# Batch 1's keys pooled by GpSimd, a new order of all steps, and no dummy matmuls, in a pooled attention and FFN kernel on one Trainium2 core

## The chip, the core and the metric

The kernel runs on one core of a Trainium2 chip. The time is the device time of one execution in microseconds (us). The engines have their own queues and run each its instructions in the order of the program: TensorE (PE, with its weight loads PEld), VectorE (DVE), ScalarE (ACT), GpSimd (POOL) and SyncE (SP, which issues the DMAs). They wait for one another by semaphores.

## The reference

Eight batches of 576 tokens with 8 heads of 64. Keys and values are pooled by means of 8, which leaves 72 of each. Softmax attention gives x; then x is normalized and goes through two matrix products with a ReLU between, and x is added.

```python
k_p = k.reshape(B, H, Sp, pool, D).mean(axis=3)
v_p = v.reshape(B, H, Sp, pool, D).mean(axis=3)
scores = scale * np.matmul(q, k_p.transpose(0, 1, 3, 2))
scores = scores - np.max(scores, axis=-1, keepdims=True)
attn = np.exp(scores)
attn = attn / (np.sum(attn, axis=-1, keepdims=True) + 1e-09)
attn_out = np.matmul(attn, v_p)
x = attn_out.transpose(0, 2, 1, 3).reshape(B, S, H * D)
mu = np.mean(x, axis=-1, keepdims=True)
var = np.mean((x - mu) ** 2, axis=-1, keepdims=True)
xn = (x - mu) / np.sqrt(var + 1e-06) * g_ln
ch = np.maximum(xn @ w_ch1, 0.0) @ w_ch2        # 512 -> 2048 -> 512
return x + ch
```

## The kernel before

The 4608 tokens are 36 tiles of 128, and 9 chunks of four tiles. For each tile, step A loads q, multiplies it with the pooled keys of the tile's batch (or of its two batches: tile 4 holds the end of batch 0 and the start of batch 1) and takes the row maxima (matmuls L788 into `ps_a`, DVE L798). For tiles 0 to 3 the steps E compute the same scores turned, half a tile at a time (PE L847 and L854, ACT exponentials L859 and L860), and POOL takes the low part of the probabilities (L862); for later tiles DVE subtracts the maxima (L803), ACT takes the exponentials, and POOL makes the low part (L824, L827). Step B multiplies the probabilities with the pooled values (matmuls L923 to L925, for later tiles L927 and L928), and DVE makes x and its mean and variance of it (L935, L943, L945, L955, L956). Then x is turned by matmuls (`parts_turned`, L876 and L884 into `ps_m`), ACT scales the result into a high part (L894) and a full copy `z` (L897), and POOL subtracts the two for the low part (L899).

Numbers that need more precision than f16 are kept as a high and a low f16 part, and a product is then three matmuls. The weights w1 and w2 are converted so in eight blocks each: C converts (ACT L532, L536, DVE L540), M1 and M2 find the scales, and S splits a block (ACT L480 the high part, DVE L487 the low one; for the first four blocks of w2 ACT L482 and POOL L484).

F is a sixteenth of a chunk's first product (`ffn_in`, L1111) with ACT and DVE making its ReLU's two parts (L1120, L1122); G is one tile of the second product (`ffn_out`, L1314, with DVE L1325 adding it to x). From chunk 2 on the first product, and from chunk 3 on the second, is done by a scheme with seven products of quarters in place of eight (`product` L1155, `out_seven` L1272); T, U, TW, WH, KW, EL, ER, ES, EP and LW make and load the sums and the parts which that scheme needs.

HK and HV load half a batch's keys and values and pool them, a pair of heads or a head at a time. `pool_k` has two branches. Keys of a batch in `K_GPSIMD` come from DRAM with the pooled index outermost, and POOL adds 4 to 4, 2 to 2 and 1 to 1 (L648, L649, two L656 straight into `kblk`); other keys are reduced by DVE (L652) and copied into `kblk` by DVE (two L658). The host lays out `kT` by the same table (L1437). Values are added by POOL (L672 to L674).

Nothing is scheduled by a planner: two strings of tokens, START and STEADY, say in which order the steps go. Each step is a generator; `run()` advances a token's generator by one stage whenever the token comes up, so the order of tokens is the order of instructions on every engine at once, and of the DMAs. START ends in chunk 1's second product; with it the first PSUM pools are closed (`ps_s` 1 buffer for scores, `ps_x` 1 for values, `ps_f` 3, `ps_m` 1).

`KEEP_BUSY` = {2: 12}: ahead of the third call of `parts_turned` (tile 2's x) 12 matmuls of the identity with itself go into the same PSUM tile (L872), which the real matmuls then overwrite.

Of the kernel before, what the change touches and what calls it, by code (L numbers as in the profile page):

```python
# [67 lines left out]
E.2.1 B.0 B.1 S.1.0 S.1.0 S.1.1 C.2.0 HK.1.0 HK.1.0 R.2.2 R.2.2 C.1.3 C.1.3 E.2.1 E.2.1 E.2.0 E.2.0 HV.1.0 HV.1.0 A.3
HK.1.1 HV.1.1 A.3 A.3 A.3 S.1.1 S.1.1 C.1.2 C.1.2 B.0 B.0 E.3.0 E.3.1 B.0 E.3.0 S.1.2 E.3.1 A.4 B.1 B.1 B.1 B.2 B.0 B.0
B.1 HK.1.0 HK.1.0 S.1.2 S.1.2 S.1.3 C.2.1 C.2.2 B.2 B.2 B.2 E.3.0 E.3.0 E.3.1 E.3.1 B.3 B.1 B.1 B.2 S.1.3 S.1.3 F.0.0.0  # L70
F.0.1.0 F.0.2.0 F.0.0.0 F.0.1.0 HK.1.1 HK.1.1 R.2.3 R.2.3 C.2.1 C.2.0 C.2.0 C.2.0 C.2.1 C.2.1 F.0.2.0 C.2.3 HK.1.1
HK.1.1 A.4 F.0.0.0 F.0.0.0 F.0.3.0 F.0.1.0 F.0.1.0 F.0.4.0 A.4 A.4 F.0.4.0 F.0.2.0 F.0.2.0 C.2.2 C.2.3 B.3 B.3 HV.1.1
HV.1.0 HV.1.0 HV.1.1 HK.2.0 A.5 D.0 D.0 A.5 F.0.5.0 B.3 F.0.5.0 F.0.3.0 C.2.2 C.2.2 C.2.3 C.2.3 B.2 B.2 B.3 HV.1.1
HV.1.1 R.1.4 R.1.4 A.4 F.0.4.0 F.0.4.0 F.0.3.0 F.0.3.0 F.0.6.0 F.0.7.0 F.0.6.0 HV.1.1 HV.1.1 A.4 A.4 R.1.5 R.1.5 R.1.6
R.1.6 R.1.7 R.1.7 A.5 A.5 F.0.7.0 F.0.5.0 F.0.5.0 B.3 B.3 M2.0 M2.0 F.0.0.1 M2.0 M2.0 S.2.0 F.0.0.1 F.0.6.0 F.0.6.0
F.0.1.1 F.0.1.1 HV.1.1 F.0.7.0 F.0.7.0 HV.1.1 HV.1.1 F.0.2.1 HV.1.1 HV.1.1 F.0.2.1 F.0.0.1 F.0.0.1 F.0.1.1 F.0.1.1
HV.1.1 HV.1.1 HV.1.1 D.1 D.1 HV.2.0 A.5 S.2.0 S.2.0 F.0.2.1 F.0.2.1 HK.2.0 HK.2.0 A.6 A.6 F.0.3.1 F.0.4.1 A.6 C.1.5
C.1.5 S.2.1 F.0.3.1 F.0.4.1 A.6 C.1.6 S.2.1 S.2.1 S.2.2 F.0.3.1 F.0.3.1 C.1.4 F.0.4.1 F.0.4.1 C.1.7 A.6 M1.1 S.2.2
S.2.2 HV.2.0 HV.2.0 A.5 A.5 HK.2.1 A.7 A.7 F.0.5.1 F.0.6.1 B.4 F.0.7.1 M1.1 F.0.5.1 C.1.4 S.2.3 F.0.6.1 F.0.7.1 C.1.6
C.1.7 A.7 A.7 C.1.5 C.1.5 F.0.5.1 F.0.5.1 C.1.4 C.1.4 R.2.4 R.2.4 A.6 A.6 R.2.5 R.2.5 S.2.3 S.2.3 B.4 F.0.6.1 F.0.6.1  # L80
HK.2.0 HK.2.0 B.4 A.7 HK.2.1 HK.2.1 HV.2.0 HV.2.0 A.8 A.8 G.0.0.0 B.5 G.0.1.0 G.0.0.0 G.0.0.0 M1.1 M1.1 S.1.4 C.2.4 B.5
B.6 F.0.7.1 F.0.7.1 G.0.2.0 G.0.3.0 C.1.7 C.1.7 S.1.4 S.1.4 S.1.5 C.2.5 C.1.6 C.1.6 R.2.6 R.2.6 C.2.4 S.1.5 S.1.5 S.1.6
C.2.4 C.2.4 G.0.1.0 G.0.1.0 A.8 A.8 HK.2.1 HK.2.1 S.1.6 S.1.6 S.1.7 C.2.6 B.4 HV.2.0 HV.2.0 R.2.7 R.2.7 HV.2.1 A.7 A.7
C.2.7 B.6 G.0.2.0 G.0.2.0 A.8 S.1.7 S.1.7 HV.2.0 HV.2.0 B.4 HV.2.1 HV.2.1 B.4 B.4 B.5 HV.2.1 HV.2.1 A.8 A.8 HV.2.1
HV.2.1 A.9 A.9 F.0.8 F.0.8 A.10 HV.3.0 A.9 A.10 F.0.9 B.7 A.11 C.2.6 C.2.6 C.2.6 C.2.5 C.2.5 C.2.5 C.2.7 C.2.7 C.2.7
F.0.9 B.5 A.9 G.0.3.0 G.0.3.0 F.0.10 F.0.10 F.0.8 F.0.8 M2.1 M2.1 F.0.11 F.0.11 B.7 B.8 F.0.9 F.0.9 F.0.12 F.0.10
F.0.10 A.9 A.9 A.9 M2.1 M2.1 S.2.4 F.0.12 HV.2.1 A.10 A.11 B.5 HV.2.1 HV.2.1 F.0.13 S.2.4 S.2.4 S.2.5 F.0.13 F.0.12
F.0.12 F.0.11 F.0.11 F.0.14 F.0.15 S.2.5 S.2.5 HV.2.1 HV.2.1 S.2.6 F.0.14 F.0.13 F.0.13 T.1.0 HV.2.1 HV.2.1 HV.2.1
HV.2.1 B.6 B.6 T.1.0 S.2.6 S.2.6 S.2.7 F.0.15 A.10 HV.3.0 HV.3.0 B.5 B.5 B.6 F.0.14 F.0.14 S.2.7 S.2.7 B.7 B.7 F.0.15
F.0.15 G.0.0.1 G.0.1.1 G.0.2.1 HV.3.0 HV.3.0 HK.3.0 B.6 B.6 G.0.0.1 T.1.0 B.7 HV.3.0 HV.3.0 G.0.0.1 G.0.0.1 B.7 B.7  # L90
HV.3.1 A.10 A.10 A.10 HK.3.0 T.1.0 A.11 A.11 HV.3.0 HV.3.0 G.0.1.1 G.0.1.1 G.0.1.1 T.1.0 T.1.0 T.1.0 B.8 B.9 G.0.3.1
HV.3.1 HV.3.1 G.0.2.1 G.0.2.1 G.0.2.1 A.11 HV.3.1 HV.3.1 A.11 A.11 B.9 V.10 F.1.0 HV.3.1 HV.3.1 HK.3.0 HK.3.1 V.10 B.11
F.1.1 F.1.1 F.1.0 T.1.0 G.0.3.1 G.0.3.1 G.0.3.1 B.8 HV.3.1 HV.3.1 HV.3.1 F.1.2 F.1.2 F.1.1 F.1.1 F.1.0 F.1.0 F.1.3
F.1.4 T.1.0 T.1.0 F.1.3 HV.3.1 F.1.2 F.1.2 F.1.5 F.1.5 F.1.4 T.1.0 T.1.0 HK.3.0 HK.3.0 T.1.1 T.1.1 F.1.3 F.1.3 F.1.6
F.1.5 F.1.5 F.1.4 F.1.4 F.1.7 T.1.1 T.1.1 T.1.1 T.1.1 F.1.6 F.1.7 B.8 T.1.1 T.1.1 F.1.7 F.1.7 F.1.6 F.1.6 G.1.0.0
G.1.1.0 G.1.2.0 T.1.1 T.1.1 T.1.1 T.1.1 G.1.0.0 G.1.0.0 G.1.3.0 T.0.0 T.0.0 T.0.0 T.0.0 T.0.0 T.0.0 HV.3.1 T.0.0 T.0.0
T.0.0 T.0.0 T.0.0 T.0.0 T.0.1 T.0.1 G.1.2.0 G.1.2.0 G.1.1.0 G.1.1.0 F.1.8 F.1.9 F.1.8 T.0.1 T.0.1 B.8 G.1.3.0 G.1.3.0
# [1363 lines left out]
```

## Time and profile before

| | us |
|---|---|
| median of three runs | 813.9 |
| the three runs | 811.84, 813.9, 815.95 |
| the profiled execution | 814.76 |
| its span on the core | 813.0 |
| granted TensorE clock, mean over the span | 0.998 |
| ACT busy | 470.7 (58%) |
| POOL busy | 487.6 (60%) |

A busy time is the sum over an engine's instructions, on the profiled execution. The profile's other views are cut by time: a table of stretches gives each engine's busy time in a stretch with the mean granted clock; the waits group an engine's idle time by what ended it; a group of instructions has the form "line engine operation out<-in count | busy us, mean ns | idle us before them"; a time line has "start, duration, engine, line, ..., [idle before <- what ended it]". Buffers are named without their numbers.

### The profile page before, as it was taken

Reading aid. Unit: us, or ns where it says so; the run is one execution under the profiler, and the core shown is the slowest. Engines: PE = TensorE matmul, PEld = TensorE weight load, DVE = VectorE, ACT = ScalarE, POOL = GpSimd, SP = SyncE. Lnnn points to the kernel's source line nnn. Section 1 sums busy time; section 2 is a strip of 40 time slices with the busy share of each in tenths; the row PEclk is TensorE's granted clock in tenths of the full one; section 3 lists DMA queues with packets and bytes.
Section 4 is the critical chain, followed back from the end, with each engine's and each line's share of the span. In section 5 each row is a group of like instructions: output and inputs, shape, how many; then the busy total and the mean of one; then the engine's idle time right before and its main releaser. Section 6 shows DMA issues by size and latency. Waiting matters only on the chain.

```text
span 813.0 us, 17388 instructions
## 1 busy us (share of the span) xinstructions
PE 782.8 (96%) x6618; PEld 609.5 (75%) x6618; DVE 664.0 (82%) x1352; ACT 470.7 (58%) x880; POOL 487.6 (60%) x601
## 2 busy tenths in 40 slices
...
GB/s 352 277 151 306 205 188 150 215 8 1 44 120 126 165 217 132 192 188 242 190 174 183 211 192 243 134 250 164 243 85 206 166 134 168 174 152 161 76 120 130
DMA packets 181507, 138.91 MB, mean 171 GB/s; under 512 B 143792, under 2 KB 151600, under 8 KB 179248
## 3 DMA queue, kind: packets, MB, share of 16 engines
...
q8 instruction: 52, 0.85, 0.4%
...
## 4 chain that ended last, share of the span: by engine, by line
PE 54%; DVE 6%; ACT 1%; DMA 1%; issue 1%; DVEq 0%; ACTq 0%
PE ps_f L1155 25%; PE ps_f L1272 25%; PE ps_a L788 2%; PE ps_f L1314 1%; DVE w L1193 1%; DMA ring<-w2s 1%; PE ps_a L927 1%; PE ps_a L928 1%; DVE ring L1185 1%; DVE x L1289 0%; DVE raw L1172 0%; DVE phl L1169 0%; DVE mx L798 0%; DVE raw L1013 0%; DVE raw L1169 0%
## 5 line engine op out<-in xcount | busy, mean ns | idle before, releaser
L1272 PE MATMUL ps_f<-ring,w 128*128 128x256 f16 x2016 | 231.5, 273 | 2.4 <-DVE w L1193 1.0
L1272 PEld LDWEIGHTS <-w 128*128 128x128 f16 x2016 | 196.4, 98 | 26.6 <-DVE w L1193 1.6
L1155 PE MATMUL ps_f<-zts,w 128*128 128x256 f16 x1680 | 206.7, 273 | 2.9 <-DVE raw L1169 1.4
L1155 PEld LDWEIGHTS <-w 128*128 128x128 f16 x1680 | 163.5, 98 | 23.7 <-issue 4.2
L1314 PE MATMUL ps_f<-w,ring 128*128 128x512 f16 x576 | 126.6, 379 | 2.6 <-DVE x L1325 2.2
L1174 ACT COPY raw<-ps_f 128x256 f32<-128x256 f32 x160 | 56.4, 373 | 91.4 <-PE ps_f L1155 80.8
L1314 PEld LDWEIGHTS <-ring 128*128 128x128 f16 x576 | 56.1, 98 | 68.9 <-issue 3.4
L1155 PE MATMUL ps_f<-zts,tsp 128*128 128x256 f16 x672 | 91.0, 273 | 1.7 <-ACT raw L1174 1.7
L1111 PE MATMUL ps_f<-zts,w 128*128 128x512 f16 (+1 forms) x480 | 86.9, 338 | 1.5 <-DVE w L487 1.4
L1191 ACT CAST w<-w 128x512 f16<-128x512 f32 x96 | 58.9, 618 | 44.6 <-POOL w L1211 24.5
L1193 POOL TENSOR_TENSOR w<-w 128x512 f16<-128x512 f32 x48 | 58.3, 1214 | 32.2 <-ACT w L1191 24.4
L1111 PEld LDWEIGHTS <-w 128*128 128x128 f16 x480 | 46.3, 98 | 37.8 <-DVE w L487 1.9
L1155 PEld LDWEIGHTS <-tsp 128*128 128x128 f16 x672 | 65.0, 98 | 10.1 <-issue 2.2
L1210 POOL TENSOR_TENSOR w<-raw 128x256 f32<-128x256 f32 x32 | 25.0, 780 | 65.5 <-ACT raw L1202 37.9
L1289 DVE SCALAR_TENSOR_TENSOR x<-ps_f,y,x 128x256 f32<-128x256 f32 (+1 forms) x84 | 42.0, 517 | 24.2 <-PE ps_f L1272 23.1
L824 POOL TENSOR_TENSOR phl<-e,phl 128x512 f16<-128x512 f32 x32 | 39.0, 1220 | 37.5 <-ACT phl L814 37.5
L1080 POOL TENSOR_TENSOR hl<-raw,hl 128x640 f16<-128x640 f32 x28 | 40.9, 1463 | 25.9 <-ACT hl L1078 25.8
L1289 DVE SCALAR_TENSOR_TENSOR x<-ps_f,cy,x 128x256 f32<-128x256 f32 (+1 forms) x84 | 42.2, 516 | 14.1 <-PE ps_f L1272 13.6
L1193 DVE TENSOR_TENSOR w<-raw,w 128x512 f16<-128x512 f32 (+1 forms) x64 | 45.0, 709 | 3.9 <-ACT w L1191 3.9
L788 PE MATMUL ps_a<-kblk,q 128*128 128x144 f32 (+1 forms) x320 | 43.3, 294 | 3.7 <-issue 2.5
L1169 DVE TENSOR_TENSOR raw<-ps_f,raw 128x256 f32<-128x256 f32 x80 | 32.2, 415 | 15.9 <-ACT raw L1174 9.4
L1120 ACT ACTIVATE ring<-ps_f 128x512 f16<-128x512 f32 (+1 forms) x40 | 19.4, 506 | 43.9 <-PE ps_f L1111 29.6
(182 smaller groups left out, 1480.3 us busy)
## 6 DMA issues: line engine op xcount, KB each, us to landing
...
```

The source lines that it names most:

```text
L788: nc.tensor.matmul(ps[r, p // 2, p % 2 * 2 * KV : (p % 2 + 1) * 2 * KV], lhsT=q[:, p, r], rhs=kblk[b % NKB][:, p, :], start=True, stop=True,)
L824: nc.gpsimd.tensor_tensor(out=ph[:, 0, :, KA:P], in0=e[:, :, 0:KA], in1=ph[:, 0, :, 0:KA], op=ALU.subtract)
L1080: nc.gpsimd.tensor_tensor(out=zhl[:, 1, :], in0=src, in1=zhl[:, 0, :], op=ALU.subtract)
L1111: nc.tensor.matmul(ps, lhsT=w[:, part, fs], rhs=zT[:, kz, cols], start=(n == 0), stop=(n == 3 * NKT - 1),)
L1155: nc.tensor.matmul(ps, lhsT=w[:, part, f * P : (f + 1) * P], rhs=z, start=m in (1, 2, 4, 5) and n == 0, stop=m in (2, 3, 4, 7) and n == 3 ...
L1169: nc.vector.tensor_tensor(out=o, in0=ps, in1=o, op=ALU.add)
L1174: nc.scalar.copy(out=o, in_=ps)
L1191: nc.scalar.copy(out=hi, in_=src)
L1193: engine.tensor_tensor(out=lo, in0=src, in1=hi, op=ALU.subtract)
L1272: nc.tensor.matmul(ps, lhsT=wt[2][:, left, part, f * HC + u * P : f * HC + (u + 1) * P], rhs=b[:, f // FPB, wp, f % FPB], start=n < 4 and ...
L1289: nc.vector.scalar_tensor_tensor(out=x, in0=ps, scalar=scale, in1=x, op0=ALU.mult, op1=ALU.add)
L1314: nc.tensor.matmul(ps, lhsT=h[:, part, i, cols], rhs=w[:, wp, j], start=(n == 0), stop=(n == 3 * NFT // 2 - 1),)
```

## The change

Three edits. The table `K_GPSIMD` gets batch 1 beside batch 2, in the kernel and so in the host's layout of `kT`. `KEEP_BUSY` goes, with its loop and its counter. And both strings of tokens are replaced by others that hold the same tokens, each as often as before (761 in START, 3398 in STEADY), in another order; lines below the strings move up by 4, below `parts_turned` by 11.

```diff
-KEEP_BUSY = {2: 12}
...
-K_GPSIMD, V_GPSIMD = (2,), (1, 2)
+K_GPSIMD, V_GPSIMD = (1, 2), (1, 2)
...
 START = """
-LN.2 LN.2 LK.0 LK.0 LK.1 LK.1 Q.0 Q.0 R.1.0 R.1.0 R.1.1 R.1.1 Q.1 Q.1 R.1.2 R.1.2 R.1.3 R.1.3 A.0 HV.1.0 LG LG R.2.0
...
+LN.2 LN.2 LK.0 LK.0 LK.1 LK.1 Q.0 Q.0 R.1.0 R.1.0 R.1.1 R.1.1 Q.1 Q.1 R.1.2 R.1.2 HV.1.0 HK.1.0 A.0 R.1.3 R.1.3 LG LG
...
-    n_turned = [0]
-
     def parts_turned(x, ln, cv, dst):
         ps = psum["ps_m"].tile([P, CH], F32, name="ps_m").rearrange("p (k c) -> p k c", k=NKT)
-        n_turned[0] += 1
-        for _ in range(KEEP_BUSY.get(n_turned[0] - 1, 0)):
-            nc.tensor.matmul(
-                ps, lhsT=ident, rhs=ident.unsqueeze(1).broadcast_to([P, NKT, P]), start=True, stop=True
-            )
         for k in range(NKT):
```

On PE, before, between the values matmuls of tile 2 and those of tile 3, with the twelve dummy pairs (L872) of which the last is shown, and the turned part of tile 2 (L876, L884):

```order
L872 LDWEIGHTS ident
L872 MATMUL ps_m<-ident 128x512
L876 MATMUL ps_m<-zts,x 128x128 x4
L884 MATMUL ps_m<-zts,ln 128x512
L923 LDWEIGHTS pt
L923 MATMUL ps_a<-vh,pt 128x65
```

The same place in the changed kernel, whose `kblk_113` and `kblk_114` are the pooled keys of batches 0 and 1:

```order
L843 MATMUL ps_f<-q,kblk_113 72x128
L850 MATMUL ps_f<-zts,mx 72x128
L784 MATMUL ps_a<-kblk_113,q 64x144
L784 MATMUL ps_a<-kblk_114,q 64x144
L784 MATMUL ps_a<-kblk_113,q 64x144
L784 MATMUL ps_a<-kblk_114,q 64x144
L784 MATMUL ps_a<-kblk_113,q 64x144
L784 MATMUL ps_a<-kblk_114,q 64x144
L784 MATMUL ps_a<-kblk_113,q 64x144
L784 MATMUL ps_a<-kblk_114,q 64x144
L865 MATMUL ps_m<-zts,x 128x128 x4
L873 MATMUL ps_m<-zts,ln 128x512
```

The dummies are gone; four pairs of tile 3's turned scores (the last of them shown) and all scores of tile 4 now stand ahead of tile 2's turned part, and behind it comes the first of F (L1100, before L1111).

On POOL, before, from the first low parts of the probabilities on (`phl_115` for tiles 0 and 2, `phl_116` for tiles 1 and 3):

```order
L862 TENSOR_TENSOR pt<-phl_115,pt 72x512
L862 TENSOR_TENSOR pt<-phl_116,pt 72x512 x2
L672 TENSOR_TENSOR vr<-vr 72x256
L673 TENSOR_TENSOR vr<-vr 72x128
L674 TENSOR_TENSOR vp<-vr 72x64
L672 TENSOR_TENSOR vr<-vr 72x256
L673 TENSOR_TENSOR vr<-vr 72x128
L674 TENSOR_TENSOR vp<-vr 72x64
L862 TENSOR_TENSOR pt<-phl_115,pt 72x512 x2
```

And in the changed kernel, where L858 is the old L862, L668 to L670 are the old L672 to L674, and L644, L645 and L652 are the additions of the keys:

```order
L858 TENSOR_TENSOR pt<-phl_115,pt 72x512
L668 TENSOR_TENSOR vr<-vr 72x256
L669 TENSOR_TENSOR vr<-vr 72x128
L670 TENSOR_TENSOR vp<-vr 72x64
L644 TENSOR_TENSOR kr<-kr 128x288
L645 TENSOR_TENSOR kr<-kr 128x144
L652 TENSOR_TENSOR kblk_114<-kr 64x72 x2
L858 TENSOR_TENSOR pt<-phl_116,pt 72x512
L644 TENSOR_TENSOR kr<-kr 128x288
L645 TENSOR_TENSOR kr<-kr 128x144
L652 TENSOR_TENSOR kblk_114<-kr 64x72 x2
```

The first two sets of keys, of four, stand between the low parts of tiles 0 and 1, and one set of values among them.

On DVE, before, from tile 0's x (L945) on, where L487 splits a block of w1 and L540 converts one:

```order
L945 TENSOR_TENSOR x<-ps_a,rs 128x512
L955 BN_STATS st<-x 128x6
L956 BN_AGGR ln<-st 128x2
L487 SCALAR_TENSOR_TENSOR w_90<-w_90,gs 128x1024
L652 TENSOR_REDUCE kr<-kr 128x72
L658 COPY kblk_114<-kr 64x72 x2
L540 SCALAR_TENSOR_TENSOR w_90<-w_90,ring 128x1024
L798 TENSOR_REDUCE mx<-ps_a 128x8
L487 SCALAR_TENSOR_TENSOR w_90<-w_90,gs 128x1024
```

And in the changed kernel from tile 0's x on (L934 is x, L794 the maxima, L483 the split):

```order
L934 TENSOR_TENSOR x<-ps_a,rs 128x512
L944 BN_STATS st<-x 128x6
L945 BN_AGGR ln<-st 128x2
L794 TENSOR_REDUCE mx<-ps_a 128x8
L483 SCALAR_TENSOR_TENSOR w_90<-w_90,gs 128x1024
L924 TENSOR_SCALAR sm<-ps_a,cv 128x8
L932 RECIPROCAL rs<-sm 128x8
L934 TENSOR_TENSOR x<-ps_a,rs 128x512
```

The reductions and copies of batch 1's keys are gone from DVE, and one split with one row of maxima is all that stands between the x of tile 0 and that of tile 1 (the last row).

More of the change, by code (lines that the diff above doesn't have):

```diff
@@ L68 @@
[L68 to L97, printed above, removed]
@@ new lines @@
+P.2.1.0.7 P.2.1.0.7 G.2.2.0 B.14 B.14 G.2.0.0 G.2.0.0 B.14 B.14 Z.14.0 WH.2.1.0 WH.2.1.1 HV.4.1 HK.4.1 HK.4.1 KW.0.2
+KW.0.2 TW.0.3.0 TW.0.3.0 TW.0.2.1 TW.0.2.1 HV.5.0 KW.1.2 KW.1.2 KW.1.0 KW.1.0 KW.0.0 KW.0.0 TW.0.3.1 TW.0.3.1 HK.4.1
+HK.4.1 TW.1.0.0 G.2.3.0 G.2.3.0 P.2.1.2.2 P.2.1.2.5 P.2.1.2.1 P.2.1.3.1 TW.1.0.0 G.2.1.0 G.2.1.0 P.2.1.3.2 TW.1.0.0
+TW.0.3.1 Z.14.0 Z.14.0 B.15 WH.2.1.0 WH.2.1.0 P.2.1.2.1 P.2.1.2.1 TW.0.3.1 P.2.1.2.5 P.2.1.2.5 TW.1.0.0 HV.4.1
+P.2.1.2.6 G.2.2.0 G.2.2.0 P.2.1.3.5 P.2.1.2.2 P.2.1.2.2 P.2.1.2.4 A.16 TS.3 WH.2.1.1 WH.2.1.1 P.2.1.3.1 P.2.1.3.1
@@ new lines @@
+ES.4.0.2 EP.4.0.2.0 ER.4.0.3 ER.4.0.3 B.20 P.4.1.0.7 P.4.1.0.7 O.4.0.0.1 P.4.1.1.1 EL.4.1.0 P.4.1.1.5 P.4.1.1.5 B.21
+HV.6.1 HV.6.1 HK.6.0 LW.4.0.2 LW.4.0.2 A.22 A.22 O.4.0.0.0 O.4.0.0.0 O.4.0.1.0 O.4.0.1.0 O.4.0.2.0 ES.4.0.2 ES.4.0.2
+EP.4.0.2.0 EP.4.0.2.0 O.4.0.0.1 O.4.0.0.1 O.4.0.1.1 O.4.0.1.1 O.4.0.2.1 B.22 P.4.1.1.3 ER.4.1.0 EP.4.0.2.1 HV.6.1
+HV.6.1 LW.4.0.4 LW.4.0.4 LW.4.0.6 LW.4.0.6 B.20 B.20 LW.4.0.5 LW.4.0.5 HK.6.1 ES.4.0.3 EP.4.0.3.0 HK.6.0 HK.6.0
+O.4.0.2.1 O.4.0.2.1 EP.4.0.2.1 EP.4.0.2.1 O.4.0.2.0 O.4.0.2.0 EP.4.0.3.0 EP.4.0.3.0 O.4.0.3.1 P.4.1.1.2 P.4.1.1.1
@@ new lines @@
+P.4.1.1.1 A.23 P.4.1.1.6 O.4.0.4.0 P.4.1.1.6 P.4.1.1.6 B.21 P.4.1.1.7 O.4.0.4.1 HV.6.1 ES.4.0.3 ES.4.0.3 EP.4.0.3.1
+A.23 A.23 A.23 A.24 B.22 EL.4.1.0 EL.4.1.0 P.4.1.1.2 P.4.1.1.2 P.4.1.1.4 P.4.1.1.4 P.4.1.1.4 P.4.1.1.3 P.4.1.1.3
+O.4.0.3.0 ES.4.1.0 EP.4.1.0.0 EL.4.1.1 B.21 B.21 B.21 LW.4.1.0 LW.4.1.0 LW.4.1.1 LW.4.1.1 HV.7.0 HV.6.1 O.4.0.4.1
+O.4.0.4.1 B.22 B.22 ER.4.1.0 ER.4.1.0 EP.4.0.3.1 EP.4.0.3.1 O.4.0.6.1 O.4.0.4.0 O.4.0.4.0 O.4.0.3.1 O.4.0.3.1 O.4.0.5.1
+O.4.0.6.0 B.23 P.4.1.1.7 P.4.1.1.7 ER.4.1.1 ES.4.1.0 ES.4.1.0 EL.4.1.1 EL.4.1.1 O.4.0.6.1 O.4.0.6.1 EP.4.1.0.0
```

564 lines of the change are left out of this document (288 added, 276 removed).

## The prediction

> **What bounds the kernel now.** I read the page first: its head, the busy times, then the table of stretches, the waits, and last the time lines at the waits found.
>
> ```profile
> span 813.0 us, 17388 instructions
> PE 782.8 (96%) x6618; PEld 609.5 (75%) x6618; DVE 664.0 (82%) x1352; ACT 470.7 (58%) x880; POOL 487.6 (60%) x601
> ```
>
> TensorE (PE) is busy for 782.8 of 813.0 us, so all that an unchanged amount of PE work can give back is 30.2 us. The table of stretches says where that lies (columns: stretch, then busy time and count on each engine, granted clock, DMA share, GB/s).
>
> ```profile
> core 0: us, PE busy (x) PEld busy (x) DVE busy (x) ACT busy (x) POOL busy (x), PEclk, DMA share, GB/s
> 20.00:60.00 40.00, 35.91 (x355) 30.10 (x353) 38.93 (x62) 34.35 (x50) 29.65 (x37) 1.00 0.64 214
> 60.00:100.00 40.00, 37.52 (x296) 25.15 (x296) 36.80 (x85) 35.38 (x50) 34.27 (x43) 1.00 0.82 257
> 100.00:120.00 20.00, 17.38 (x93) 9.27 (x92) 19.38 (x30) 16.96 (x25) 17.23 (x22) 0.91 0.79 195
> 111.00:114.50 3.50, 2.97 (x11) 2.36 (x12) 3.50 (x4) 3.06 (x5) 3.42 (x3) 0.51 0.49 117
> 120.00:230.00 110.00, 109.85 (x569) 51.50 (x568) 88.90 (x155) 36.22 (x60) 54.65 (x58) 1.00 0.36 85
> 230.00:330.00 100.00, 93.47 (x703) 63.28 (x701) 86.23 (x182) 45.14 (x91) 59.76 (x86) 1.00 0.69 156
> 330.00:813.00 483.00, 476.25 (x4558) 423.39 (x4556) 383.42 (x818) 295.57 (x602) 290.67 (x351) 1.00 0.64 174
> ```
>
> From 120 to 230 PE has 0.15 us of idle time: that stretch gives nothing. PE idles 4.09 us in 20 to 60, 2.48 in 60 to 100, 2.62 in 100 to 120, 6.53 in 230 to 330 and 6.75 in the last 483. From 20 to 60 VectorE (DVE) is busy 38.93 of 40 us: there it sets the pace. And for 3.5 us after 111 PE ran at a granted clock of 0.51: work done there at half speed would have taken half as long, so some 1.7 us more are lost in it.
>
> ```profile
> PE ps_a L788 <- issue: 2.5, 2, 1.3
> PE ps_m L876 <- DVE x L945: 1.7, 2, 1.2
> ```
>
> These are the two longest of PE's waits from 20 to 125 (total, times, longest). The time line has them, and one more, at two places that the change touches, the third turned part and the eighth block of w1 (the bracket gives the idle time ahead of a row and what ended it):
>
> ```profile
> 42.84 2.75 PE L872 MATMUL ps_m<-ident 128*128 128x512 bf16 x12 [0.63 <-ACT z L897]
> 46.82 1.16 PE L876 MATMUL ps_m<-zts,x 128*128 128x128 f32 x8 [1.23 <-DVE x L945]
> 109.96 0.39 PE L1111 MATMUL ps_f<-zts,w 128*128 128x512 f16 x1 [1.44 <-DVE w L487]
> 111.53 2.26 PE L788 MATMUL ps_a<-kblk,q 128*128 128x144 f32 x8 [1.18 <-issue]
> ```
>
> **The change, first 60 us.** DVE loses the four reductions and the eight copies of batch 1's keys.
>
> ```profile
> L658 DVE COPY kblk<-kr 64x72 f32<-64x72 f32 x8 | 3.3, 412 | 0.2
> L652 DVE TENSOR_REDUCE kr<-kr 128x72 f32<-128x576 f32 x4 | 2.9, 736 | 0.0
> ```
>
> That is 3.3 + 2.9 = 6.2 us off the engine that sets the pace. The x for which the third turned part waits ended just before 46.82; with some 5 us less ahead of it (what the new order puts in front of it takes back about one), it ends near 41.8.
>
> The dummies by themselves cost nothing: they filled 2.75 us of a pause that ran to 46.82 for that x. Where they go and DVE is 5 us earlier, the pause is gone as well, if PE has other work. The new order gives it: ahead of the third turned part stand half a tile of turned scores and the scores of tile 4.
>
> ```profile
> 34.77 0.38 PE L847 MATMUL ps_f<-q,kblk 128*72 128x128 f32 x2
> 36.30 0.38 PE L854 MATMUL ps_f<-zts,mx 128*72 128x128 f32 x2
> 53.48 1.38 PE L788 MATMUL ps_a<-kblk,q 128*64 128x144 f32 x16
> ```
>
> From 34.77 to 36.30 are seven steps, so a step takes 0.22 us and the eight of a half tile 1.75; the scores take 1.38. That is 3.13 us of work moved forward. If nothing holds PE, it goes through the third turned part 3.13 us after its last values matmul instead of 4.6 us after (from 42.84 - 0.63 = 42.2, the end of the values matmuls ahead of it, to 46.82), with 3.13 us of later work done.
>
> What can hold it is GpSimd (POOL). The scores of tile 4 need all of batch 1's pooled keys, and these now come from POOL, behind six subtractions L862, three sets of V additions and one L899. A key set is priced where POOL does it already, for batch 2:
>
> ```profile
> 92.83 0.80 POOL L648 TENSOR_TENSOR kr<-kr 128x288 f32<-128x288 f32 x1
> 93.70 0.48 POOL L649 TENSOR_TENSOR kr<-kr 128x144 f32<-128x144 f32 x1
> 94.27 0.72 POOL L656 TENSOR_TENSOR kblk<-kr 64x72 f32<-64x72 f32 x2
> 95.07 1.62 POOL L672 TENSOR_TENSOR vr<-vr 72x256 f32<-72x256 f32 x1
> 20.86 1.15 POOL L862 TENSOR_TENSOR pt<-phl,pt 72x512 f16<-72x512 f32 x1 [18.76 <-ACT pt L860]
> 53.55 0.73 POOL L672 TENSOR_TENSOR vr<-vr 72x256 f32<-72x256 f32 x1
> 55.15 0.36 POOL L823 MEMSET phl<- 128x320 f16 x1
> ```
>
> A set runs from 92.83 to 95.07, 2.24 us; a V set from 53.55 to 55.15, 1.6. Quiet, the queue up to the last key set is 6 x 1.15 + 3 x 1.6 + 4 x 2.24 + 1.2 = 21.9 us from 20.86, so 42.8: before PE gets there (42.2 + 1.75 = 43.95). But POOL is slower when other engines are dense:
>
> ```profile
> L862 POOL TENSOR_TENSOR pt<-phl,pt 72x512 f16<-72x512 f32 x8 | 11.0, 1392 | 21.3 <-ACT pt L860 21.3
> L672 POOL TENSOR_TENSOR vr<-vr 72x256 f32<-72x256 f32 x8 | 6.8, 848 | 0.5 <-DMA vr<-in_v_dram 0.5
> L899 POOL TENSOR_TENSOR zts<-z,zts 128x512 f16<-128x512 f32 x4 | 4.8, 1199 | 3.9 <-ACT z L897 3.9
> L673 POOL TENSOR_TENSOR vr<-vr 72x128 f32<-72x128 f32 x8 | 4.5, 566 | 0.6
> L674 POOL TENSOR_TENSOR vp<-vr 72x64 f32<-72x64 f32 x8 | 4.3, 533 | 0.6
> L648 POOL TENSOR_TENSOR kr<-kr 128x288 f32<-128x288 f32 x1 | 1.2, 1246 | 0.0
> ```
>
> These are the groups of POOL from 20 to 72. By their means an L862 takes 1.39, a V set 0.85 + 0.57 + 0.53 = 1.95, and the one L648 among them 1.246 where the quiet one took 0.80, so a key set about 3.5. The queue is then 8.4 + 5.9 + 14.0 + 1.2 = 29.5 us and ends at 50.4. The old POOL also waited 21.3 - 18.76 = 2.5 us for ScalarE in there; if that stays, it ends at 52.9.
>
> The break-even: the third turned part may start at 46.82 + 3.13 = 49.95 without loss, so the scores 1.38 earlier, at 48.6. Quiet gives 42.8, loaded 50.4. I take the middle, 46.6, since DVE, the dense neighbour, is lighter by a sixth: a gain of 2.0. Set against that is a clock halved once more as at 111, 1.7 us at one chance in three, so 0.6: about **-1.5 us**. Bounds: all idle time and the dummies' gone, -(4.09 + 2.75) = -6.8; loaded, with the wait and the half clock, 52.9 - 48.6 + 1.7 = +6.0.
>
> **60 to 120 us.** At 109.96 PE waited 1.44 us for the low part of w1's eighth block, and at 111.53 another 1.18 us for the buffer of the scores, which DVE empties; after these two the clock was 0.51. The profile names nothing for the second ("issue"), but the scores have one buffer, and it is DVE that empties it. So I put all three down to DVE being late:
>
> ```profile
> 42.45 3.22 DVE L487 SCALAR_TENSOR_TENSOR w<-w,gs 128x1024 f16<-128x1024 f32 x1
> 41.20 2.27 POOL L862 TENSOR_TENSOR pt<-phl,pt 72x512 f16<-72x512 f32 x2
> 43.43 1.15 POOL L899 TENSOR_TENSOR zts<-z,zts 128x512 f16<-128x512 f32 x1
> 108.62 1.28 DVE L487 SCALAR_TENSOR_TENSOR w<-w,gs 128x1024 f16<-128x1024 f32 x1
> ```
>
> In the new order DVE has nearly the whole 6.2 us less ahead of that split, four times the wait. At most 1.44 + 1.18 + 1.7 = 4.3 us come back. But ScalarE (35.38 of 40 us from 60 to 100) and POOL (34.27) are nearly as dense as DVE (36.80), and POOL gets the four key sets, 9 to 14 us, in return; a second product that waits for POOL's or ScalarE's parts of w2 would eat the lead. **-2.5 us**, bounds -4.3 and 0.
>
> The same lines show a price that the change raises. The split at 42.45 took 3.22 us while POOL worked through L862 and L899, the one at 108.62 took 1.28. Each addition that goes to POOL can hold up a DVE operation so; that is in the loaded end of the first term. The Trainium skill, "SBUF — State Buffer", section "Who interferes with whom", says that a DVE operation with two inputs in SBUF and a GpSimd operation that reads SBUF exclude each other for a whole instruction, while a reduction on trn2 never contends. The trace agrees in the 3.22 against 1.28. It speaks against the move: a reduction that disturbs nobody goes, and additions that block come. By it the first term would be 50.4 - 48.6 = +1.8 in place of -1.5; this is the slower rival below.
>
> **230 us to the end.** The second order table is new throughout; PE's idle time here is 6.53 + 6.75 us. The largest single wait:
>
> ```profile
> 326.95 5.34 PE L1314 MATMUL ps_f<-w,ring 128*128 128x512 f16 x24 [2.23 <-DVE x L1325]
> ```
>
> DVE is busy 86.23 of 100 us there; in the new order a little less of its work stands ahead of the densest place, 250 to 300. I take **-1 us**; bounds: most of the 6.53 gone, -5, and two more waits like this one, +4.5.
>
> **The sum.** -1.5 - 2.5 - 1 = -5.0 on the profiled execution's 814.76 us: 809.8. The median of the three times, 813.9, lies 0.86 lower, so 808.9, given as **809.0**. About 0.5% (4.1 us) is what a measurement of this kernel can tell from no change: faster means under 809.8, slower over 818.0.
>
> **The rivals.** *No change*: DVE's lead is eaten. For it: from 60 to 100 ScalarE and POOL are as dense as DVE, so that a lead of DVE is worth only what its two partners allow; against: the two longest waits name DVE. Then the first term stays and half of the second, the third is nought: 813.9 - 1.5 = about 812.5; with any half clock 814. It includes that removing the dummies does nothing, since they filled a wait. *Slower*: POOL becomes what PE waits for at tile 4's scores. For it: loaded sets end at 50.4, past the break-even of 48.6; against: POOL had idle time and DVE, which slows it, is lighter. Price: 1.8 to 4.3 us of waiting and 1.7 of half clock, and since everything behind is later too, DVE's lead at w1's eighth block is lost: 813.9 + 3.5 to 6.0, about 819. It decides from the point where key sets take over 3.0 us each with the rest as loaded (48.6 - 20.86 - 15.5 = 12.2, over four).
>
> The half clock is a part of that. PE ran at 0.51 from 111 to 114.5 after pauses of 1.44 and 1.18 us with 0.39 us of work between. The Trainium skill, "TensorE: Matmul & The Clock Gate", section "Part 1: The HAM clock gate (the "warmup" mystery)", puts the drop after an idle window of about 3.4 us; here less than that was enough. By the rule a pause of 4.6 us without dummies halves the clock for one window, and a filled one does not.
>
> **How the numbers follow.** Forecast 0.5; no change 0.33; slower 0.17. The range 803.0 to 817.5: below, the first two terms at two thirds of their bounds and the third at its middle (-4.5 - 3.5 - 3 = -11); above, the slower rival short of its middle, where a tenth is left out. The same cases give faster 0.5, same 0.33, slower 0.17.
>
> **What would show it.** Right: PE idles under 2 us from 40 to 50, its scores of tile 4 start by 46.6, L1111 does not wait for the eighth L487, and the clock stays at 1.00 to 120. Wrong: PE waits at tile 4's scores for POOL's last key addition; the clock drops near 45; L1314's first product waits for POOL's or ScalarE's part of w2; or new waits after 230 where there were none.

## The result, and the profile after

The changed kernel took 824.61 us (median of 4, 822.92 to 827.10) against 814.11 for the kernel before: a ratio of 1.0131, 95% interval 1.0101 to 1.0161. It is 10.5 us slower. The forecast was 809.0 with a range up to 817.5, so the result lies outside it, and on the other side of the kernel before. The profiled execution took 825.07 us with a span of 823.4.

The table of stretches of the changed kernel (columns as in the prediction's), with two stretches of half clock added behind:

```profile
core 0: us, PE busy (x) PEld busy (x) DVE busy (x) ACT busy (x) POOL busy (x), PEclk, DMA share, GB/s
20.00:60.00 40.00, 31.10 (x300) 26.08 (x299) 32.68 (x51) 29.76 (x41) 38.04 (x51) 0.91 0.62 215
60.00:100.00 40.00, 34.37 (x281) 25.81 (x279) 35.05 (x68) 35.23 (x52) 31.71 (x40) 0.96 0.91 252
100.00:120.00 20.00, 17.78 (x99) 8.60 (x98) 19.32 (x29) 15.42 (x19) 16.92 (x19) 1.00 0.56 169
120.00:230.00 110.00, 106.84 (x569) 50.52 (x568) 91.79 (x161) 38.70 (x66) 57.76 (x62) 1.00 0.37 86
230.00:330.00 100.00, 96.71 (x710) 63.81 (x709) 82.35 (x180) 45.09 (x90) 56.67 (x78) 1.00 0.62 149
330.00:824.00 494.00, 484.39 (x4599) 427.31 (x4596) 396.09 (x832) 296.79 (x607) 300.56 (x361) 1.00 0.62 173
48.70:55.60 6.90, 6.45 (x23) 4.23 (x24) 4.80 (x4) 4.72 (x8) 6.68 (x8) 0.51 0.36 140
82.90:86.30 3.40, 3.40 (x19) 2.42 (x17) 3.33 (x4) 3.39 (x5) 2.72 (x4) 0.50 1.13 210
```

From 20 to 60 us DVE went from 38.93 busy to 32.68, as the edit says, and POOL from 29.65 to 38.04 of 40. The engine that set the pace was relieved and another took its place; PE's busy time fell by 4.8 us. Where the 10.4 us of span went, as PE's idle time and half of the time at half clock, in each stretch:

| stretch | before | after | difference | forecast |
|---|---|---|---|---|
| 20 to 60 | 4.09 idle + 2.75 dummies | 8.90 idle + 3.4 clock | +5.5 | -1.5 |
| 60 to 120 | 5.10 idle + 1.7 clock | 7.85 idle + 1.7 clock | +2.8 | -2.5 |
| 120 to 230 | 0.15 | 3.16 | +3.0 | 0 |
| 230 to the end | 13.28 | 12.3 | -1.0 | -1 |

That is +10.3. The stretches are cut by time and not by work, so that one or two us stand in the wrong row: counted at points where both kernels have done the same matmuls (shown under "The second loss"), PE is 3.6 us late by the fourth turned part, at 60 us, and 8.2 us late 20 us further on.

PE's longest waits from 20 to 125, in the changed kernel:

```profile
PE ps_a L784 <- POOL kblk L652: 5.1, 1, 5.1
PE ps_f L1100 <- DVE ring L1111: 3.0, 2, 2.1
PE ps_a L913 <- POOL pt L858: 1.6, 1, 1.6
```

The two waits of before at this place (for x and for w1's split) are gone. Ahead of them all now stands one on POOL's last addition of batch 1's keys. Here it is on PE's time line, with the half clock behind it:

```profile
42.82 1.19 PE L784 MATMUL ps_a<-kblk,q 128*64 128x144 f32 x14
49.15 0.74 PE L784 MATMUL ps_a<-kblk,q 128*64 128x144 f32 x2 [5.14 <-POOL kblk L652]
49.82 2.08 PE L865 MATMUL ps_m<-zts,x 128*128 128x128 f32 x8
...
53.40 1.91 PE L1100 MATMUL ps_f<-zts,w 128*128 128x256 f16 x8
```

and on POOL's, from its last work ahead of that set:

```profile
42.22 0.72 POOL L668 TENSOR_TENSOR vr<-vr 72x256 f32<-72x256 f32 x1
43.02 0.45 POOL L669 TENSOR_TENSOR vr<-vr 72x128 f32<-72x128 f32 x1
43.55 1.34 POOL L670 TENSOR_TENSOR vp<-vr 72x64 f32<-72x64 f32 x1
44.84 0.18 POOL L952 COPY ln<-cv 128x2 f32<-128x2 f32 x1
44.98 1.15 POOL L888 TENSOR_TENSOR zts<-z,zts 128x512 f16<-128x512 f32 x1
46.09 0.78 POOL L644 TENSOR_TENSOR kr<-kr 128x288 f32<-128x288 f32 x1
46.95 1.35 POOL L645 TENSOR_TENSOR kr<-kr 128x144 f32<-128x144 f32 x1
48.37 0.72 POOL L652 TENSOR_TENSOR kblk<-kr 64x72 f32<-64x72 f32 x2
```

POOL has no pause in there. The set ends at 49.1: 6.3 us after the quiet sum of the prediction (42.8) and 1.3 before the loaded one (50.4). The L645 that took 1.35 stood beside a DVE split of 3.32 us; another, at 27.44 beside a reduction on DVE, took 0.49.

The second place is the time line at 82.53, in front of the other half clock: PE's product waits 2.09 us for DVE's ReLU parts.

```profile
82.53 4.45 PE L1100 MATMUL ps_f<-zts,w 128*128 128x256 f16 x24 [2.09 <-DVE ring L1111]
```

```profile
78.39 1.22 DVE L536 SCALAR_TENSOR_TENSOR w<-w,raw 128x1024 int32<-128x1024 int32 x1
79.52 2.62 DVE L483 SCALAR_TENSOR_TENSOR vb<-vp,sv,vh 72x512 f16<-72x512 f32 x1
82.06 0.74 DVE L1111 SCALAR_TENSOR_TENSOR ring<-ps_f,ring 128x256 f16<-128x256 f32 x2
```

In the second fence (DVE's time line) those parts stand behind a conversion and the split of batch 1's V.

### The profile page after: what moved, and what is told of

Its sections match the earlier page's. It is cut to its first block, busy times and chain, and to the rows that moved or that the text cites. A ratio compares the mean times of both kernels' runs of the same rounds, so it can differ in the third digit from the quotient of the medians.

```text
span 823.4 us, 17338 instructions
## 1 busy us (share of the span) xinstructions
PE 784.1 (95%) x6606; PEld 609.7 (74%) x6606; DVE 667.6 (81%) x1340; ACT 468.7 (57%) x880; POOL 503.0 (61%) x617
## 4 chain that ended last, share of the span: by engine, by line
PE 66%; DVE 24%; POOL 3%; ACT 3%; issue 2%; DMA 1%; DVEq 0%; POOLq 0%
PE ps_f L1144 25%; PE ps_f L1261 23%; PE ps_f L1303 6%; PE ps_f L1100 5%; DVE w L536 2%; PE ps_a L784 2%; DVE w L1182 2%; DVE raw L611 2%; DVE ring L1174 1%; DVE w L483 1%; DVE mx L794 1%; DVE ring L1111 1%; DVE x L1278 1%; DVE x L1314 1%; PE ps_a L916 1%
## 5 line engine op out<-in xcount | busy, mean ns | idle before, releaser
L1100 PE MATMUL ps_f<-zts,w 128*128 128x512 f16 (+1 forms) x480 | 88.9, 344 | 6.8 <-DVE ring L1111 4.7
L1182 POOL TENSOR_TENSOR w<-w 128x512 f16<-128x512 f32 x48 | 59.4, 1238 | 48.2 <-ACT w L1180 30.3
L1100 PEld LDWEIGHTS <-w 128*128 128x128 f16 x480 | 48.0, 101 | 45.1 <-issue 8.4
L784 PEld LDWEIGHTS ps_a<-kblk,q 128*128 128x128 f32 (+1 forms) x320 | 37.4, 180 | 11.4 <-POOL kblk L652 5.4
L1182 DVE TENSOR_TENSOR w<-raw,w 128x512 f16<-128x512 f32 (+1 forms) x64 | 42.1, 660 | 3.0 <-ACT w L1180 3.0
```

What stands on the lines that cost most here:

```text
L784: nc.tensor.matmul(ps[r, p // 2, p % 2 * 2 * KV : (p % 2 + 1) * 2 * KV], lhsT=q[:, p, r], rhs=kblk[b % NKB][:, p, :], start=True, stop=True,)
L1100: nc.tensor.matmul(ps, lhsT=w[:, part, fs], rhs=zT[:, kz, cols], start=(n == 0), stop=(n == 3 * NKT - 1),)
L1182: engine.tensor_tensor(out=lo, in0=src, in1=hi, op=ALU.subtract)
```

## The experiments

The first theory of the loss was that the four key sets overfill POOL's queue, so that all that PE gets from POOL up to 60 us comes late. The rivals were that the new order is bad whoever pools the keys, that the missing dummies cost the clock, and that the second string loses. Ratios are against the kernel before, run beside each; in brackets the 95% interval.

| kernel | median us | ratio |
|---|---|---|
| changed | 824.61 | 1.0131 [1.0101, 1.0161] |
| changed, keys back on DVE | 827.02 | 1.0165 [1.0133, 1.0197] |
| before, keys on POOL | 819.17 | 1.0078 [1.0052, 1.0105] |
| before, no dummies | 816.54 | 1.0043 [1.0027, 1.0058] |
| before, keys on POOL and no dummies | 820.25 | 1.0081 [1.0063, 1.0099] |
| changed, second string of before | 824.92 | 1.0134 [1.0100, 1.0168] |
| changed, dummies in the wait | 823.43 | 1.0125 [1.0109, 1.0141] |
| changed, last key set earlier on POOL | 825.07 | 1.0145 [1.0129, 1.0161] |
| changed, tile 4's scores later | 828.60 | 1.0191 [1.0175, 1.0207] |
| changed, low part on DVE | 826.48 | 1.0135 [1.0116, 1.0153] |
| before, keys on POOL, low part on DVE | 817.98 | 1.0035 [1.0021, 1.0050] |
| the same without dummies | 821.05 | 1.0060 [1.0039, 1.0081] |
| changed, ReLU parts first | 825.58 | 1.0129 [1.0113, 1.0144] |
| changed, last key set on DVE | 823.67 | 1.0119 [1.0092, 1.0147] |
| before, one key set on POOL | 811.89 | 0.9976 [0.9962, 0.9990] |
| changed, shortened maxima | 821.13 | 1.0087 [1.0063, 1.0110] |
| before, shortened maxima | 813.80 | 0.9999 [0.9984, 1.0015] |

### The three edits apart

Keys back on DVE, in the changed kernel:

```diff
-K_GPSIMD, V_GPSIMD = (1, 2), (1, 2)
+K_GPSIMD, V_GPSIMD = (2,), (1, 2)
```

> The changed kernel with batch 1's keys given back to DVE (the new order and no dummies stay). Theory, POOL's queue: the four key sets on POOL are what tile 4's scores waited for (5.1 us) and what halved the clock behind it; without them the wait at those scores falls below 2 us, the clock stays at 1.00 from 40 to 60, and the time is 5 to 8 us under the changed kernel, 817 to 820. Rival, the order itself is bad: PE waits there for DVE instead, within 3 us of the changed kernel, 822 to 825.

Measured 1.0165: no gain. The wait for POOL's keys is gone from PE's waits, and the longest are now

```profile
PE ps_f L850 <- DVE mx L794: 5.1, 2, 3.0
PE ps_f L1100 <- DVE w L483: 3.5, 3, 1.5
```

The rival's mechanism came out, with a time above its 822 to 825: with this order and the keys on DVE, DVE is the one that is late. The new order is slow whoever pools the keys (1.0165 and 1.0131, the intervals overlap).

Keys on POOL alone, in the kernel before:

```diff
-K_GPSIMD, V_GPSIMD = (2,), (1, 2)
+K_GPSIMD, V_GPSIMD = (1, 2), (1, 2)
```

> The kernel before with batch 1's keys on POOL alone (old order, dummies kept). Theory, POOL's queue: the key sets push POOL's low parts ahead of the first product back, so the old order loses too, 2 to 5 us, 816 to 819, though its scores of tile 4 stand late. Rival, only the place of tile 4's scores was wrong: 0 to 2 us are gained, since DVE has 6.2 us less to do, 812 to 814.

Measured 1.0078, 6 us slower, a little over what the theory gave. One row each of PE's, ScalarE's and POOL's time line, and the stretch from 40 to 60, tell how:

```profile
44.92 5.10 PE L872 MATMUL ps_m<-ident 128*128 128x512 bf16 x12 [2.80 <-ACT z L897]
```

```profile
44.19 0.69 ACT L897 ACTIVATE z<-ps_m,cv 128x512 f32<-128x512 f32 x1 [3.50 <-POOL zts L899]
```

```profile
43.01 1.15 POOL L899 TENSOR_TENSOR zts<-z,zts 128x512 f16<-128x512 f32 x1
```

```profile
40.00:60.00 20.00, 15.70 (x141) 10.76 (x142) 10.15 (x15) 12.74 (x18) 18.76 (x29) 0.83 0.30 97
```

A key set ahead of it made POOL's low part of tile 0 (L899) 3 us late. It reads `z`, which has one buffer, so ScalarE's next z waited; that z is what frees `ps_m`, also one buffer, and PE waited for that. The dummies then ran at half clock, 5.10 us for what took 2.75. DVE has only 10.15 us of work in 20 us: the relief is there and nobody can use it.

No dummies, in the kernel before:

```diff
-KEEP_BUSY = {2: 12}
+KEEP_BUSY = {}
```

> The kernel before without the twelve dummies, nothing else changed. Theory: they filled a wait, so the pause of 4.6 us stays and ends at the same 46.8; either nothing (814), or the clock is halved behind it for one window, +1.7 (815.6). Rival, the dummies are what the change lost: +4 or more, 818 or over.

Measured 1.0043, 3.5 us, between the two. The pause, as its third turned part shows, stayed:

```profile
47.05 2.04 PE L876 MATMUL ps_m<-zts,x 128*128 128x128 f32 x8 [4.68 <-ACT w L480]
```

and that part took 2.04 us where it took 1.16 with the dummies: the clock was 0.50 from 46.8 to 50.2. In the timed runs the mean clock was 0.992 to 0.998; in the runs of before beside them 0.994 to 1.000, mostly 1.000. One such window of 3.4 us takes 0.002 off the mean, so the median of 0.994 stands for about three (an estimate), and that is most of the 3.5 us: the one run of before with a mean of 0.994 took 817.15 too. Costing the dummies at nothing was wrong: they filled a wait, and bought the clock behind it.

Both small edits in the old order:

> The kernel before with both small edits, batch 1's keys on POOL and no dummies, in the old order. In the run with the keys on POOL alone the dummies came after the wait (44.92, 5.10 us at half clock) and held PE up. Theory, the new order itself carries most of the loss: without them the third turned part starts near 45, and the time is 814 to 818. Rival, the two edits add up (6.2 + 3.6) and the order gives nothing: 821 to 825.

Measured 1.0081. Neither number: the edits don't add up; a likely reason is that the second takes dummies away which the first had pushed behind the wait. The two small edits give 6.6 us of the loss, more than half. What the new order puts on top is 1.0131 - 1.0081 = 0.5%, 4 us, known only to some 3 us.

The second string of before, in the changed kernel:

> The changed kernel with the second order string of before. In the trace PE of the changed kernel is 9.2 us late at 120 us and 10 us at the end. Theory, the loss is in the first 120 us: 823 to 825, within 1.5 us of the changed kernel. Rival, the second string loses by itself: 818 to 820.

Measured 1.0134 against 1.0131: no part of the second string in it can be seen, so what the order loses comes with the first string.

### Is it that one wait?

Four kernels take away the 5.1 us wait, or what it does, each in another way. Dummies in the wait:

```diff
+            for _ in range(70 if t == TPC and p == NPAIR - 1 else 0):
+                nc.tensor.matmul(
+                    ps[:, 1, 4 * KV : 4 * KV + P], lhsT=ident, rhs=ident, start=True, stop=True, skip_group_check=True
+                )
             for r, b in segments(t):
                 nc.tensor.matmul(
```

> The changed kernel with 70 dummy matmuls of 128x128 ahead of the last pair of tile 4's scores, in the 5.1 us wait, into columns of the tile that nobody reads. Theory, half of the loss there is the clock, which the wait halves for 6.8 us: the wait stays, the clock is 1.00 up to 60, the time 3 to 5 us lower, 819.5 to 821.5. Rival, the clock is a by-product that DVE and POOL hide anyway: 823 to 825.

Measured 1.0125. The clock did stay up, 0.996 to 1.000 in the timed runs against 0.991 to 0.994 of the changed kernel. The ratio fell by 0.06%, 0.5 us, which is known only to some 3 us; the span in the trace is 1.8 us shorter. So the 3 to 5 us of the theory did not come, and the clock is at most a small part of the loss: PE at full speed still waits 2.10 us for DVE's late ReLU parts.

```profile
44.70 4.08 PE L784 MATMUL ps_a<-ident 128*128 128x128 bf16 x70
...
80.09 4.06 PE L1104 MATMUL ps_f<-zts,w 128*128 128x256 f16 x24 [2.10 <-DVE ring L1115]
```

The last key set earlier on POOL (tokens of START, the second pair of HK.1.1 moved ahead of HV.1.0 and B.0):

```diff
-... E.2.1 E.2.1 HK.1.1 HK.1.1 HV.1.0 HV.1.0
+... E.2.1 E.2.1 HK.1.1 HK.1.1 HK.1.1 HK.1.1 HV.1.0 HV.1.0
...
-... B.0 B.0 HK.1.1 HK.1.1 E.3.0 E.3.0 B.1 B.1 B.2 ...
+... B.0 B.0 E.3.0 E.3.0 B.1 B.1 B.2 ...
```

> The changed kernel with the additions of the last key set moved on POOL ahead of the third set of V and of tile 0's low part, about 4 us earlier; its keys were loaded 12 us before. Theory, POOL's queue at tile 4's scores: the wait falls from 5.1 to 1 to 2 us, the clock stays up behind it, 820 to 822. Rival, the low part that is moved back holds PE up instead (ScalarE's single z buffer): 824 or more.

Measured 1.0145; the rival came true. On PE's time line the wait for the keys is 2.22, and behind it is a new one, for z:

```profile
46.78 0.74 PE L784 MATMUL ps_a<-kblk,q 128*64 128x144 f32 x2 [2.22 <-POOL kblk L652]
50.45 2.08 PE L865 MATMUL ps_m<-zts,x 128*128 128x128 f32 x8 [2.93 <-ACT z L886]
```

The sum, 5.15 us, is no less than the old 5.14.

Tile 4's scores later (three A.4 moved behind the first two F and B.3):

> The changed kernel with tile 4's scores moved behind the third turned part, the first two products and tile 3's values. Theory, POOL is late as a whole there: PE then waits at the first product for POOL's low part of tile 1 (it ended at 51.6), so at most 2.5 us come back, 822 to 824. Rival, only the place of the scores was wrong: PE goes on at 45, the clock stays up, 816 to 819.

Measured 1.0191, worse than the theory gave. The profile names what it named, and z as well:

```profile
47.05 2.08 PE L865 MATMUL ps_m<-zts,x 128*128 128x128 f32 x8 [4.00 <-ACT z L886]
...
52.80 2.50 PE L1100 MATMUL ps_f<-zts,w 128*128 128x256 f16 x11 [1.75 <-POOL zts L888]
```

The last key set on DVE (the table and the host's layout by pair; pairs 0 to 2 on POOL):

> The changed kernel with the last of batch 1's four key sets pooled by DVE, the other three by POOL. Theory, the wait for that set is worth its length: DVE has the set by 46, the wait at tile 4's scores falls from 5.1 to under 2 us, POOL's low part of tile 1 is 2 to 3 us earlier, 819 to 822. Rival, POOL's queue as a whole sets the pace and PE waits at the next place for it: 823.5 to 825.5.

Measured 1.0119, inside the rival's range, its interval overlapping that of the changed kernel. The wait for the keys is gone from the list; 3.7 us for DVE's splits and 1.9 for z stand there.

So the 5.1 us were the place at which POOL's queue was met first. In the three kernels that took them away PE waits about as long at the next things that POOL or DVE owes it.

### Can the queue be relieved?

If the lateness reaches PE through z, then DVE taking chunk 0's low part from PSUM (no z copy, no L899) should help:

```diff
-Z_LO = "pool"
+Z_LO = "dve"
```

> The old order with batch 1's keys on POOL and the dummies kept, and in addition the low part of the turned x of chunk 0 taken by DVE straight from PSUM: no z copy on ScalarE, no L899 on POOL, four operations of some 0.75 us more on DVE. Theory, POOL's lateness reaches PE through the single z buffer (ScalarE waited 3.50 us for L899, and PE 2.8 us for z): both waits go, the dummies end by 45 at full clock, 811 to 815. Rival, DVE cannot take it or POOL's other work (probabilities' low parts, V) holds PE as much: 817 to 820.

Measured 1.0035, 817.98 us: 0.4% better than with POOL's low part, less than the theory gave and within the rival's range. PE no longer waits for z, but 2.9 us for the low part itself, which now holds `ps_m` until DVE gets to it:

```profile
PE ps_m L876 <- DVE zts L902: 3.8, 2, 2.1
PE ps_m L872 <- DVE zts L902: 2.9, 1, 2.9
```

> The same without the dummies. Theory as above: the 2.8 us for z and the 1.5 us for POOL's low part go, against 820.3 for the same order with the low part on POOL: 814 to 817; if the clock is halved in the pause that stays, 817. Rival: 819 to 821.

Measured 1.0060, and single runs from 815.71 to 822.22: a miss for the theory, whose upper end was 817. Those of mean clock 0.991 or 0.992 lie above 820, those of 0.996 and 0.998 below 817.

> The changed kernel with that low part on DVE. Here PE waits for the last key set and not for z, and one L899 of 1.15 us stood ahead of it. Theory, POOL's queue: the wait goes from 5.1 to about 4, the time 1 to 3 us under the changed kernel, 822 to 824. Rival, the whole loss came through z: 816 to 819.

Measured 1.0135: no gain. Theory and rival both missed. PE now waits 7.0 us for that low part on DVE (L891).

One key set on POOL in place of four, in the kernel before with its dummies. The table goes by pair:

```diff
-K_GPSIMD, V_GPSIMD = (2,), (1, 2)
+K_GPSIMD, V_GPSIMD = ((1, 1), (2, 0), (2, 1), (2, 2), (2, 3)), (1, 2)
...
-        if b in K_GPSIMD:
+        if (b, p) in K_GPSIMD:
```

> The kernel before, dummies kept, with one key set (the second pair's, which stood ahead of the third x on DVE) on POOL in place of four. Theory, POOL has room for one set but not for the first and all four: DVE's third x comes 2 us earlier, 811.5 to 814. Rival, each set costs the same quarter of 6.2 us: 815 to 816.

Measured 0.9976 [0.9962, 0.9990], 2 us faster than the kernel before, as the theory had it, and the one version that beats both kernels. Two and three sets were not run in the old order. The set moved is the one that stood on DVE right ahead of the x for which the third turned part waits. On PE's time line:

```profile
41.63 2.75 PE L872 MATMUL ps_m<-ident 128*128 128x512 bf16 x12 [0.63 <-ACT z L897]
44.21 1.05 PE L876 MATMUL ps_m<-zts,x 128*128 128x128 f32 x8
...
47.52 3.98 PE L1111 MATMUL ps_f<-zts,w 128*128 128x256 f16 x35 [0.55 <-POOL zts L899]
```

Against before, where that part began 1.23 us after the dummies, it follows them at once. The 0.55 us for POOL's low part behind it say how little room was left on POOL.

### The second loss, at 80 us

DVE's two ReLU parts ahead of what stood in front of them (in START, F.0.3.1 and F.0.4.1 moved ahead of A.6, C.1.4 and HV.1.1):

> The changed kernel with DVE's two ReLU parts (L1111), for which PE waited 2.09 us at 82.53 before the clock fell, moved ahead of tile 6's maxima, a conversion and the split of V of batch 1. Theory, the second loss, 4 us at 80 to 86, is this place of the new order: the pause and the half clock behind it go, 820.5 to 822.5. Rival, DVE is simply full there (19.37 of 20 us), so the wait turns up at the next place: 824 to 826.

Measured 1.0129; the rival. The wait for those parts is gone and one ahead of the scores is in its place. The profile names nothing for it ("issue"); the scores have one buffer, and DVE empties it:

```profile
81.39 1.22 PE L784 MATMUL ps_a<-kblk,q 128*128 128x144 f32 x8 [2.49 <-issue]
82.45 4.45 PE L1100 MATMUL ps_f<-zts,w 128*128 128x256 f16 x24
```

Less work for DVE in that stretch, in both kernels:

```diff
-                in_=src,
+                in_=src if b < WB // 2 else src[:, 0:64],
```

> The changed kernel with the maxima of w1's last four blocks (L520 at 65 to 85 us, 1.2 us each) taken over 64 of each row's 1024 elements, so that part of the reduction is left out. Theory, the second loss at 79 to 93 us is DVE being full: 4 to 4.5 us of DVE work less ahead of it gives 2.5 to 4.5 us, 820 to 822. Rival, PE's waits there come from POOL or ScalarE: 823.5 to 825.

> The same shortened maxima in the kernel before. Its DVE is as full from 80 to 120 (38.3 of 40 us), and PE waited there for DVE by 1.44 and 1.18 us: at most 2.6 us come back, 811 to 813. If the gain is as large as in the changed kernel, DVE's load is no mark of the change; if it is nothing, ScalarE and POOL set the pace there.

Measured 1.0087 in the changed kernel, 0.44% or 3.6 us less than 1.0131 (known to some 3 us), and 0.9999 in the kernel before. The same DVE work costs nothing before, and some 3 us after. In the run of the shortened maxima PE is busy 17.53 us from 60 to 80 and 19.19 from 80 to 100, where it was 18.58 and 15.79 in the changed kernel; the 2.1 us wait for the ReLU parts stayed. DVE idled in the changed kernel for 8.5 us from 40 to 80 (31.46 of 40 busy), waiting for what PE, POOL and ScalarE had late, and from 80 to 120 it is full (38.69 of 40).

Is the second loss the first one's debt, or the new order's own? The traces can tell. When the fourth turned part begins, and again when the L467 at 79.78 begins (L463 after the change), both kernels have done the same matmuls, the dummies aside. So the difference of these starts is how late PE is. Before:

```profile
60.43 1.13 PE L876 MATMUL ps_m<-zts,x 128*128 128x128 f32 x8 [0.51 <-DVE x L945]
79.78 0.22 PE L467 MATMUL ps_m<-ident,rowmax 128*128 128x128 bf16 x1
```

and in the changed kernel:

```profile
64.03 1.06 PE L865 MATMUL ps_m<-zts,x 128*128 128x128 f32 x8
87.96 0.23 PE L463 MATMUL ps_m<-ident,rowmax 128*128 128x128 bf16 x1
```

| kernel | late at the fourth turned part, us | late at the L467 | lost between |
|---|---|---|---|
| changed | 3.6 | 8.2 | 4.6 |
| changed, dummies in the wait | 1.0 | 5.6 | 4.6 |
| changed, keys back on DVE | 5.0 | 8.9 | 3.9 |
| changed, tile 4's scores later | 6.7 | 12.1 | 5.4 |
| before, keys on POOL | 4.5 | 4.8 | 0.3 |
| before, keys on POOL and no dummies | 5.2 | 5.2 | 0.0 |

The six other kernels with the new first string lose 3.8 to 5.2 us between the two points, the five others with the old one -0.2 to 1.5. So the second loss comes with the order of the new first string, however late PE was before and whoever pools the keys; it is not the first one's debt. (The first column varies by 1.5 us between kernels that are the same up to there, so it is the rougher one.) What in that order costs it is open. ScalarE has no pause there (the columns are those of the table of stretches, first before, then after):

```profile
60.43:79.78 19.35, 18.87 (x180) 15.78 (x181) 17.25 (x44) 19.19 (x31) 14.61 (x22) 1.00 0.96 313
64.03:87.96 23.93, 20.42 (x182) 16.82 (x181) 19.51 (x42) 23.72 (x36) 18.60 (x24) 0.93 0.82 254
```

For the same matmuls 4.5 us more of ScalarE's work stand between the two points, among it one block more of w2's split. No run took work off ScalarE there, and with the ReLU parts first it was busy 22.17 of 24.41 us and the loss stayed. So it is not shown that ScalarE is the cause.

## Why the prediction was wrong

**What bounds.** Right that DVE set the pace up to 60 us and that PE's idle time is all there is to gain. It missed that POOL was no second best: its 10 us of pauses were waits for ScalarE ahead of work that others need at once, and work put into the queue delays what is behind it.

**First term, -1.5; measured +5.5 by time, +3.6 by equal work.** This step failed, in POOL's queue and in the break-even. It priced the queue between 42.8 and 50.4 and took the middle, 46.6, because DVE would be lighter. The queue ended at 49.1, at a time when DVE was lighter by 6 us: from 20.00 it took 29.1 us, where the loaded rows gave 29.5. The rows had the right price; the choice of the middle had no row behind it.

The break-even of 48.6 was too late. It counted 3.13 us of work moved ahead of the third turned part, 1.75 of them half a tile of turned scores. But in the kernel before all turned scores stand ahead of it too; the last of them is done ahead of the second one:

```profile
37.61 0.38 PE L854 MATMUL ps_f<-zts,mx 128*72 128x128 f32 x2
39.50 1.13 PE L876 MATMUL ps_m<-zts,x 128*128 128x128 f32 x8 [1.50 <-ACT w L480]
```

Only the 1.38 us of tile 4's scores were moved, so the third turned part had to start by 48.2 and not by 49.95, and even the middle would have gained next to nothing. It started at 49.82, 1.6 us late, and the half clock lay on it. DVE's side of the step held: the third x ended at 42.66, where some 41.8 was forecast. Two signs of being wrong that the prediction names came: PE waited at tile 4's scores for POOL's last key addition, and the clock fell behind it, at 48.7.

The step looked also at one consumer only, the scores of tile 4. POOL's low parts, z and `ps_m` were never priced, and they are why moving the scores or the last key set gave nothing.

**The dummies at nothing.** Wrong by 3.5 us in the old order. That they filled a wait was right. That a half clock came at one chance in three was not: without them every timed run had a lower mean clock than 1.000.

**The half clock, 1.7 us.** In the changed kernel it was two windows at the first place (6.9 us at 0.51) and one at the second. But keeping it up gave 0.5 us by the ratios and 1.8 by the traces, so as a part of the loss the 1.7 was not too small.

**60 to 120 us, -2.5; measured +2.8, and +3.0 more up to 230.** This step failed as well. The old waits for w1's split shrank from 1.44 to 0.9 us. DVE's lead of 6 us was gone before it got there: it turned into idle time from 40 to 80. And the term priced that lead alone, and nothing that the new order itself puts into the stretch; that order lost 4.6 us by equal work from 60 to 80 us of the kernel before.

**230 us to the end, -1; measured -1.0.** The number is right. Putting the second string back changed nothing that could be seen (1.0134 against 1.0131), so the reason given for it is not shown, and this may be luck.

**The rivals.** The slower one had the mechanism and the place, and a chance of 0.17. Its price, 819, was half of the loss, because it ended with the wait and the clock. No rival had the new order itself as slow, which gives the other part. What the Trainium skill's "SBUF — State Buffer", section "Who interferes with whom", was quoted for, two inputs from SBUF on DVE against GpSimd's reads, is seen again in the L645 of 1.35 us beside a split and 1.50 beside a conversion, against 0.49 beside a reduction. The sentence on it gave +1.8 for the first term, nearer than the sum.

**The range.** Two thirds of the second term's bound of -4.3 are -2.9, not -3.5; the lower end would have been 803.5. It does not touch the outcome.
